# Linear attention with a routed feed-forward block on one core: two first loads exchanged between two DMA queues

## The chip, the cores and the metric

The kernel runs on one core of a Trainium2 chip. The core has a matrix engine (TensorE, PE in the profile), a vector engine (VectorE, DVE), a scalar engine (ScalarE, ACT), a general engine (GpSimd, POOL) and a synchronisation engine (SyncE, SP). The engines run their own instruction streams and wait for one another by semaphores. Transfers between the chip's memory and the core's SBUF are issued by an engine on its own DMA queue and carried by 16 DMA engines. The metric is the device time in microseconds; a version counts by the median of its runs.

## The reference

```python
x = A_x                                   # 1 x 2048 x 640, bf16
xn = _layernorm(x, axis=-1)
return x + _A_ref(xn, wqkv, wo) + _B_ref(xn, w_r, w_gate, w_up, w_down)

# _A_ref: linear attention, 32 heads of 20
q, k, v = split(xn @ wqkv)
phi = lambda t: where(t > 0, t + 1, exp(t)) + 1e-6
kv = einsum("bhsd,bhse->bhde", phi(k), v); z = phi(k).sum(s)
o = (phi(q) @ kv) / (phi(q) . z + 1e-6)
return o.reshape(B, S, D) @ wo

# _B_ref: the 8 rows with the largest xn @ w_r go through a gated feed-forward block
r = xn @ w_r;  idx = argsort(-r)[:8]
y = (silu(x_sel @ w_gate) * (x_sel @ w_up)) @ w_down * sigmoid(r_sel)
return xn + scatter_add(y at idx)
```

## The kernel before

The 2048 rows of x are 16 tiles of 128 rows. A tile of x is 128 x 640 in bf16, 160 KB. The kernel first runs through the tiles: normalise a tile (`ln_a`, `ln_b`: the two halves of the statistics on VectorE, lines 151 and 154; `ln_g`: their aggregate, line 157; `ln_r`: the inverse deviation by a logarithm and an exponential on ScalarE, lines 160 and 161; `ln_xn`: the normalised tile on VectorE, line 165), turn it, multiply it by the k columns of `wqkv` (`K`, line 208), apply phi (lines 224, 227, 243) and accumulate phi(k) times the normalised tile over all tiles (`G`, lines 248 and 253). Afterwards come q, the small matrices per head, the routed rows and the output.

Tiles 0 to 3 are turned on TensorE (`tr_mm`, line 174) and copied out of PSUM (`tr_cp`, line 181 on ScalarE, line 183 on VectorE). Later tiles are turned by a DMA (`tr_dma`). The order of the work on every engine is written out by hand: an engine does its instructions in the order in which the program names them.

The k columns come in two halves of 320, each 128 x 5 x 320 in SBUF and 400 KB: `wkh[0]` and `wkh[1]`. Each product of a tile with a half is five matmuls. Behind the columns of `wkh[1]` stands one column for the router weights `wr`: they are loaded as 5 rows of 128, transposed on TensorE (line 133) and copied by ScalarE (line 135), so that r comes out of the same products as k.

TensorE's first instructions, ahead of the first transposes of x, are filler products of a constant zero (`warm4`, line 121): one 512 wide, one 256 wide, then the transpose of `wr`, then another 512 wide. The filler of 32-bit numbers shows as two passes each.

What the change touches are the first loads, all issued through `ld` (line 103), so that the profile shows line 103 for every one. SyncE's queue holds x of tiles 0, 1, 2 and 3, then `wkh[1]`, then three loads of four tiles each. ScalarE's queue holds the table load of its functions (line 106), `wr` and `wkh[0]`. A transfer is not waited for by the engine that issues it; its users wait for its landing.

```python
ld(sp, XX[:, 0, 1, :], x_v[:, 0, :])
act.preload_act_table_set("natural_log_exp_and_others")
...
ld(act, wr[:], B_w_r.rearrange("(kc p) -> kc p", p=P))
ld(act, wkh[0], wqkv_v[:, :, D : D + HW])
ld(sp, XX[:, 1, 1, :], x_v[:, 1, :])
```

Of the kernel before, what the change touches and what calls it, by code (L numbers as in the profile page):

```python
# [9 lines left out]
D = 640  # L10
# [28 lines left out]
def kernel(  # L39
# [13 lines left out]
    pe, dve, act, pool, sp = nc.tensor, nc.vector, nc.scalar, nc.gpsimd, nc.sync  # L53

    x_v = A_x[0].rearrange("(t p) d -> p t d", p=P)
    out_v = out[0].rearrange("(t p) d -> p t d", p=P)
    wqkv_v = A_wqkv.rearrange("(kc p) n -> p kc n", p=P)
# [9 lines left out]
    def st(shape, dt, name, tag=None):  # L67
        return sb.tile(shape, dt, name=name, tag=tag or name)

    XX = st([P, T, 2, D], BF16, "XX")  # L70
# [27 lines left out]
    HW = 320  # L98
    wkh = [wk[:, :, 0:HW], wk[:, :, HW + 64 :]]


    def ld(eng, dst, src):
        eng.dma_start(dst, src)
# [3 lines left out]
    dve.memset(zero[:], 0.0)  # L107
    dve.memset(MVf[:], 0.0)
    wr = st([KC, P], BF16, "wr")
    ld(act, wr[:], B_w_r.rearrange("(kc p) -> kc p", p=P))  # L110
    ld(act, wkh[0], wqkv_v[:, :, D : D + HW])
    ld(sp, XX[:, 1, 1, :], x_v[:, 1, :])
    ld(sp, XX[:, 2, 1, :], x_v[:, 2, :])
    ld(sp, XX[:, 3, 1, :], x_v[:, 3, :])
    ld(sp, wkh[1][:, :, 0:HW], wqkv_v[:, :, D + HW : 2 * D])
# [824 lines left out]
```

## Time and profile before

| What | us |
|---|---|
| three runs: median, lowest, highest | 107.11, 106.8, 107.3 |
| the profiled execution | 106.82 |
| its span, first to last instruction | 105.1 |
| TensorE busy | 101.2 |
| VectorE busy | 82.3 |
| ScalarE busy | 69.3 |

The profile divides the span into instructions by engine. A row of the timeline gives the start, the time until the end of the last instruction that it merges, the engine, the line and the operation, the tiles written and read, the number of instructions, and in brackets the idle time before it with what ended that. PEld stands for the loads of a matrix into the array, which run beside products; SPq and ACTq are the issuing parts of SyncE and ScalarE. XX is the tile buffer of x, wk holds both halves of the k weights. In the tables of stages the columns are the stretch, its length, then busy time and number of instructions of PE, PEld, DVE, ACT and POOL, the granted clock of TensorE, the busy share of the DMA engines and GB/s. Queue q1 is SyncE's and q10 ScalarE's.

A busy TensorE row is no proof of full pace, since the ends of products are modelled; the starts are recorded.

### The profile page before, as it was taken

How to read it: one execution, taken by the hardware profiler on the slowest of the kernel's cores; microseconds unless marked ns; L12 is line 12 of the kernel's file. 1: busy time of each engine (PE TensorE's matmuls, PEld its weight loads, DVE VectorE, ACT ScalarE, POOL GpSimd, SP SyncE). 2: the span in 40 equal slices, each digit the busy share in tenths (PEclk: the TensorE clock that was granted, in tenths of full speed). 3: DMA queues.
4: the chain of work that ended last, by engine and by line, in shares of the span. 5: the costliest groups of instructions: out<-in, count | busy, mean ns of one | idle time of the engine just before them, and what ended most of it. 6: DMA issues, size and time to landing. Idle time of an engine off the chain costs nothing.

```text
span 105.1 us, 2557 instructions
## 1 busy us (share of the span) xinstructions
PE 101.2 (96%) x924; PEld 63.3 (60%) x924; DVE 82.3 (78%) x187; ACT 69.3 (66%) x171; POOL 17.3 (16%) x60
## 2 busy tenths in 40 slices
PE   6999999999999999999999999999999999999980
PEld 3346666666666666667556555655567767777760
DVE  1787999988888897873788985728988997888870
ACT  4289957666666666888596999969993997000000
POOL 7800000620000000000000683300002300000500
DMA  2899937334655765889998999921730125895343
GB/s 76 231 356 386 306 68 62 72 66 90 141 124 115 109 131 128 180 252 354 264 404 264 288 337 378 360 66 50 242 119 9 29 95 200 175 369 205 125 128 125
DMA packets 23024, 19.65 MB, mean 187 GB/s; under 512 B 10595, under 2 KB 21475, under 8 KB 23011
## 3 DMA queue, kind: packets, MB, share of 16 engines
q1 hardware_dynamic: 21880, 19.01, 62.6%
q10 hardware_dynamic: 842, 0.46, 1.8%
q8 instruction: 7, 0.11, 0.5%
q0 software_dynamic: 288, 0.01, 0.3%
q14 instruction: 7, 0.05, 0.2%
HBM read 13.80 MB, written 3.65 MB: 166 GB/s over the span
## 4 chain that ended last, share of the span: by engine, by line
PE 90%; DMA 5%; DVE 1%; issue 1%; ACT 1%; DVEq 0%
PE PS L208 21%; PE PS L474 21%; PE PS L739 20%; PE PS L248 16%; DMA wk<-in_A_wqkv_dram 5%; PE PS L253 3%; PE PS L695 2%; PE PS L655 1%; PE PS L538 1%; PE PS L717 1%; PE PS L267 1%; PE PS L174 1%; PE PS L666 1%; DVE o L752 1%; PE PS L618 1%
## 5 line engine op out<-in xcount | busy, mean ns | idle before, releaser
L208 PE MATMUL PS<-wk,xnT 128*128 128x320 bf16 (+1 forms) x160 | 25.3, 300 | 0.1
L248 PE MATMUL PS<-pk,XX 128*128 128x512 bf16 x80 | 23.5, 379 | 0.0
L474 PE MATMUL PS<-xnT,wq 128*128 128x512 bf16 x100 | 22.6, 380 | 0.0
L739 PE MATMUL PS<-Mb,pqT 128*128 128x320 bf16 (+4 forms) x165 | 22.1, 295 | 0.0
L224 ACT ACTIVATE ek<-PS 128x320 bf16<-128x320 f32 x32 | 14.1, 441 | 9.9 <-PE PS L208 9.9
L739 PEld LDWEIGHTS <-pqT 128*128 128x128 bf16 x165 | 15.9, 98 | 6.4 <-issue 0.3
L208 PEld LDWEIGHTS <-xnT 128*128 128x128 bf16 x160 | 15.3, 98 | 6.6 <-ACT xnT L181 0.2
L474 PEld LDWEIGHTS <-wq 128*128 128x128 bf16 x100 | 11.4, 118 | 9.1 <-issue 0.2
L243 DVE SCALAR_TENSOR_TENSOR pk<-ek,rk 128x640 bf16<-128x640 bf16 x16 | 13.1, 820 | 4.8 <-ACT rk L227 4.5
L529 DVE SCALAR_TENSOR_TENSOR pqT<-qe,qr 128x512 bf16<-128x512 bf16 x20 | 13.5, 683 | 2.1 <-ACT qr L481 2.0
L480 ACT ACTIVATE qe<-PS 128x512 bf16<-128x512 f32 x20 | 12.2, 609 | 3.3 <-PE PS L474 3.3
L253 PE MATMUL PS<-pk,XX 128*128 128x128 bf16 x64 | 14.0, 219 | 0.0
L227 ACT ACTIVATE rk<-PS 128x320 bf16<-128x320 f32 x32 | 14.0, 437 | 0.0
L248 PEld LDWEIGHTS <-XX 128*128 128x128 bf16 x80 | 7.8, 98 | 8.1
L481 ACT ACTIVATE qr<-PS 128x512 bf16<-128x512 f32 x20 | 12.2, 608 | 0.0
L748 DVE TENSOR_TENSOR o<-PS,XX 128x640 bf16<-128x640 f32 x11 | 9.0, 822 | 2.9 <-issue 1.3
L198 ACT ACTIVATE XX<-XX,MR,SR 128x640 bf16<-128x640 bf16 x11 | 9.4, 913 | 0.0
L151 DVE BATCH_NORM_STATS2 stats<-XX 128x6 f32<-128x320 bf16 x16 | 7.4, 461 | 2.2 <-DMA XX<-in_A_x_dram 2.2
L259 POOL MEMSET XX<- 128x1 bf16 x18 | 2.0, 117 | 35.4 <-DVE XX L165 15.2
L165 DVE TENSOR_SCALAR XX<-XX,MVf,SR 128x640 bf16<-128x640 bf16 (+2 forms) x17 | 7.2, 431 | 0.6 <-ACT SR L161 0.6
L154 DVE BATCH_NORM_STATS2 stats<-XX 128x6 f32<-128x320 bf16 x16 | 7.7, 480 | 0.0
L253 PEld LDWEIGHTS <-XX 128*128 128x128 bf16 x64 | 6.3, 98 | 0.8
(113 smaller groups left out, 95.3 us busy)
## 6 DMA issues: line engine op xcount, KB each, us to landing
out_dram<-o SPq DMA_DIRECT2D x15, 160.0 KB, 2.4
XX<-in_A_x_dram SPq DMA_DIRECT2D x3, 640.0 KB, 6.9
wg<-in_B_w_gate_dram SPq DMA_DIRECT2D x5, 384.0 KB, 9.0
wu<-in_B_w_up_dram SPq DMA_DIRECT2D x5, 384.0 KB, 6.2
wd<-in_B_w_down_dram SPq DMA_DIRECT2D x1, 1920.0 KB, 11.1
wv<-in_A_wqkv_dram SPq DMA_DIRECT2D x5, 160.0 KB, 3.0
wq<-in_A_wqkv_dram SPq DMA_DIRECT2D x1, 800.0 KB, 5.3
hi_d<-XX SPq DMA_DIRECT2D x1, 800.0 KB, 4.0
```

The source lines that it names most:

```text
L198: act.activation(XX[:, t, 1, :], XX[:, t, 1, :], AF.Identity, bias=MR[:, t : t + 1], scale=SR1[:, t : t + 1])
L208: pe.matmul(PS[:, b + h, off(t, h) : off(t, h) + w], lhsT=xnT[:, kc, t * P : (t + 1) * P], rhs=wkh[h][:, kc, 0:w], start=(kc == 0), stop=( ...
L224: act.activation(phis[t][0][:, h * HW : (h + 1) * HW], phi_src(t, h, b), AF.Exp)
L227: act.activation(phis[t][1][:, h * HW : (h + 1) * HW], phi_src(t, h, b), AF.Relu)
L243: dve.scalar_tensor_tensor(out=pk[:, t, :], in0=ek[:], scalar=1.0, in1=rk[:], op0=ALU.min, op1=ALU.add)
L248: pe.matmul(PS[:, a, :], lhsT=lhsT, rhs=pk[:, t, 0:512], start=(t == 0), stop=(t == T - 1),)
L253: pe.matmul(PS[:, 5, a * P : (a + 1) * P], lhsT=lhsT, rhs=pk[:, t, 512:D], start=(t == 0 and a == 0), stop=(t == T - 1), skip_group_check= ...
L474: pe.matmul(PS[:, bank, :], lhsT=by5(wq[:, kc, :])[:, m, :], rhs=xnT[:, kc, tb * TBLK : (tb + 1) * TBLK], start=(kc == 0), stop=(kc == KC ...
L480: act.activation(e, PS[:, bank, :], AF.Exp)
L481: act.activation(r, PS[:, bank, :], AF.Relu)
L529: dve.scalar_tensor_tensor(out=pqT[:, m, tb * TBLK : (tb + 1) * TBLK], in0=e, scalar=1.0, in1=r, op0=ALU.min, op1=ALU.add,)
L739: pe.matmul(PS[:, b, o : o + c1 - c0], lhsT=pqT[:, kc, t * P : (t + 1) * P], rhs=Mb[:, kc, c0:c1], start=(kc == 0), stop=(kc == KC - 1))
```

## The change

Three lines are written differently. x of tile 1 becomes the first transfer on ScalarE's queue, and `wr` the second. `wkh[0]` moves from ScalarE's queue to the second place on SyncE's, where x of tile 1 was. Nothing else differs, and the bytes are the same.

```diff
     wr = st([KC, P], BF16, "wr")
+    ld(act, XX[:, 1, 1, :], x_v[:, 1, :])
+    ld(sp, wkh[0], wqkv_v[:, :, D : D + HW])
     ld(act, wr[:], B_w_r.rearrange("(kc p) -> kc p", p=P))
-    ld(act, wkh[0], wqkv_v[:, :, D : D + HW])
-    ld(sp, XX[:, 1, 1, :], x_v[:, 1, :])
     ld(sp, XX[:, 2, 1, :], x_v[:, 2, :])
```

The head of ScalarE's stream, with what leaves it and what comes in (XX is x of tile 1, wk the first half of the k weights):

```order
 L935 UNCONDITIONAL_BRANCH
 L106 ACT_TABLE_LOAD
+L103 DMA XX<-in_A_x_dram 128x640
 L103 DMA wr<-in_B_w_r_dram 5x128
-L103 DMA wk<-in_A_wqkv_dram 128x5x320
 L135 COPY wk<-PS 128x5
```

The router weights are second now, and no weights of k are issued here.

The head of SyncE's stream; the four tiles that stood in one row are parted by the weights:

```order
 L935 UNCONDITIONAL_BRANCH
-L103 DMA XX<-in_A_x_dram 128x640 x4
+L103 DMA XX<-in_A_x_dram 128x640
+L103 DMA wk<-in_A_wqkv_dram 128x5x320
+L103 DMA XX<-in_A_x_dram 128x640 x2
 L103 DMA wk<-in_A_wqkv_dram 128x5x320
 L103 DMA XX<-in_A_x_dram 128x4x640 x3
```

The first half of the k weights stands behind tile 0 and ahead of tiles 2 and 3. The streams of TensorE, VectorE and GpSimd are the same in both kernels.

## The prediction

> **What bounds the kernel now.** I read the busy shares and the 40 slices first, then the chain of waits from the start, then the timeline of the first 10 us on each engine.
>
> ```profile
> PE 101.2 (96%) x924; PEld 63.3 (60%) x924; DVE 82.3 (78%) x187; ACT 69.3 (66%) x171; POOL 17.3 (16%) x60
> PE   6999999999999999999999999999999999999980
> 1.47 5.10 DMA wk<-in_A_wqkv_dram
> 6.57 0.04 issue
> 6.61 0.43 PE PS L208 x2
> 7.04 0.17 PE PS L174 x3
> 7.21 1.70 PE PS L208 x12
> ```
>
> TensorE is busy in every slice from the second on, and the chain from 6.61 us onward consists of TensorE pieces without a break. Before 6.61 it is the landing of the first half of the k weights, issued on ScalarE's queue at 1.47 and landed at 6.57. What the program can gain or lose by a new order of its first loads is therefore the moment at which TensorE's unbroken stretch begins, and whatever small holes follow until about 10 us. From there to 55 us nothing can absorb a shift:
>
> ```profile
> 6.60:10.00 3.40, 3.39 (x29) 2.15 (x28) 2.77 (x9) 3.05 (x12) 0.33 (x2) 1.00 1.06 377
> 10.00:55.00 45.00, 45.00 (x325) 28.45 (x325) 37.46 (x93) 33.16 (x100) 3.53 (x22) 1.00 0.70 170
> ```
>
> The second number of a row is its length, the third TensorE's busy time: 45.00 of 45.00. So I treat a shift at 10 us as a shift of the end, one for one.
>
> But the weights are not the only thing that stands just before 6.61. The chain names the last of several arrivals; the others are close behind:
>
> ```profile
> 3.17 0.49 DVE L151 BATCH_NORM_STATS2 stats<-XX 128x6 f32<-128x320 bf16 x1 [1.91 <-DMA XX<-in_A_x_dram]
> 3.97 0.48 DVE L151 BATCH_NORM_STATS2 stats<-XX 128x6 f32<-128x320 bf16 x1
> 5.16 1.05 DVE L165 TENSOR_SCALAR XX<-XX,MVf,SR 128x256 bf16<-128x256 bf16 x3
> 5.56 0.11 PEld L174 LDWEIGHTS <-XX 128*128 128x128 bf16 x2 [1.27 <-DVE XX L165]
> 5.89 1.10 ACT L181 COPY xnT<-PS 128x256 bf16<-128x256 bf16 x3 [0.16 <-PE PS L174]
> 6.33 0.10 PEld L208 LDWEIGHTS <-xnT 128*128 128x128 bf16 x1
> 6.54 0.49 DVE L151 BATCH_NORM_STATS2 stats<-XX 128x6 f32<-128x320 bf16 x1 [0.34 <-DMA XX<-in_A_x_dram]
> ```
>
> This is the chain of tile 0: x of tile 0 lands and VectorE starts its statistics at 3.17 after 1.91 us of waiting for it; the normalised tile comes at 5.16 and after; the first transpose follows at 5.56, its copy at 5.89, and the first k weight load into the array is done from 6.33. The product needs that load, 0.10 long, at least in part, so it could have started between 6.33 and 6.43; I take 6.39. The k weights therefore cost only 6.61 - 6.39 = 0.22 us (0.18 to 0.28). The second row matters as much: x of tile 1 shows no idle time before it, so nobody waited for that transfer. The last row shows x of tile 2, which did cost 0.34 us of VectorE.
>
> **The change, part by part.** The order of work on TensorE, VectorE and GpSimd is the same; only the first loads move. SyncE's transfers keep their places but for the second, where half of the k weights stands for x of tile 1. On ScalarE two transfers remain, x of tile 1 first. No step waits on more than before, and no issue becomes slower: the SyncE issues took about 0.43 us each for a tile and for half of the weights alike.
>
> ```profile
> 0.81 1.82 SPq L103 DMA_DIRECT2D XX<-in_A_x_dram  x4
> 0.84 0.59 ACTq L103 DMA_DIRECT2D wr<-in_B_w_r_dram  x1
> 1.27 0.42 SPq L103 DMA_DIRECT2D XX<-in_A_x_dram  x1
> 1.47 0.41 ACTq L103 DMA_DIRECT2D wk<-in_A_wqkv_dram  x1
> 2.67 0.43 SPq L103 DMA_DIRECT2D wk<-in_A_wqkv_dram  x1
> ```
>
> So x of tile 1 is issued at 0.84 instead of 1.27, the k weights at 1.27 instead of 1.47, the router weights at about 1.43 instead of 0.84. What the transfers then do to each other is read from this table of stages, whose last two columns are the busy share of the 16 DMA engines and GB/s:
>
> ```profile
> 1.70:2.60 0.90, 0.90 (x2) 0.34 (x1) 0.00 (x0) 0.39 (x1) 0.90 (x2) 1.00 0.73 209
> 2.60:3.10 0.50, 0.50 (x2) 0.34 (x1) 0.00 (x0) 0.00 (x0) 0.50 (x4) 1.00 1.01 271
> 3.10:3.60 0.50, 0.50 (x2) 0.00 (x0) 0.43 (x2) 0.00 (x0) 0.42 (x2) 1.00 0.47 90
> 3.60:4.60 1.00, 1.00 (x3) 0.60 (x3) 1.00 (x5) 0.18 (x2) 0.83 (x4) 1.00 0.90 215
> 4.60:6.60 2.00, 1.88 (x9) 0.46 (x8) 1.63 (x6) 1.71 (x6) 0.66 (x3) 1.00 1.09 347
> ```
>
> Added up, 0.188 MB have moved by 2.60, 0.324 by 3.10, 0.369 by 3.60, 0.584 by 4.60.
>
> *Tile 0 loses its head start: +0.40.* A tile of x is 0.164 MB. Before, it goes first and nearly alone, so it is through at about 1.70 + 0.164/0.209 = 2.49, and VectorE starts 0.68 later, at 3.17. Now tile 1 is issued 0.03 after it on the other queue. If the two alternate, both are through when 0.328 MB have moved, at about 3.14, and with the same 0.68 VectorE starts at 3.82: 0.65 later. If SyncE's packets all went first, it would be 0. Which of these is nearer is told by a stage in which both queues had work:
>
> ```profile
> q10 hardware_dynamic: 216, 0.14, 65.2%
> q1 hardware_dynamic: 63, 0.08, 24.8%
> ```
>
> These are packets, MB and share from 3.60 to 4.60 (q1 is SyncE's queue, q10 ScalarE's): neither is held back behind the other, so I go nearer to alternation than to no delay, but below its full price, since the pair need not both end at its last packet: 0.40, with 0 and 0.65 kept as ends. The Trainium skill, page "DMA: Bandwidth & Descriptors", section "Issuing engines are not separate DMA queues", says the same against this change: transfers started by different engines run on the same 16 DMA engines and interleave, and a second issuer saves only the time of issuing. By that rule the second queue brings tile 1 no bandwidth that tile 0 does not lose; the rows just shown agree.
>
> *The wait for the k weights goes: -0.22.* They are now behind 0.328 MB of x: 0.738 MB are through at 4.60 + (0.738 - 0.584)/0.347 = 5.04. Even with 1 us to land, that is ahead of the 6.79 (6.39 + 0.40) at which TensorE will ask for them. What hides this transfer is tile 0's own chain; without that cover the wait would return, since the landing now is 6.57.
>
> *x of tile 2: 0.* It has 0.902 MB up to its end, 5.52 by the same sum, 6.5 with the same 1 us. VectorE, which works through tiles 0 and 1 first (busy until 6.21 now, 6.61 then), will not wait for it. The 0.34 us that it waits now is where 0.34 of the 0.40 is taken up on VectorE; but TensorE and ScalarE, which start tile 0's products and copies later, are not helped by that.
>
> *Router weights: 0 to +0.5, taken as covered.* They move from the front of ScalarE's queue behind 0.164 MB. TensorE's queue holds their transpose ahead of a last filler product and of all transposes of x:
>
> ```profile
> 3.67 0.10 PEld L133 LDWEIGHTS <-wr 5*128 5x128 bf16 x1 [0.65 <-issue]
> 3.79 1.78 PE L121 MATMUL PS<-const-float32-0.0 128*128 128x512 f32 x2
> 4.80 0.77 PE L121 MATMUL PS<-const-float32-0.0 128*128 128x512 f32 x1
> 5.56 0.99 PE L174 MATMUL PS<-ident,XX 128*128 128x128 bf16 x7
> ```
>
> The transpose ran at 3.67 without a wait for data, and the filler behind it ends with the first transpose's start at 5.56: there is no slack in it. If the router weights land at 3.82, like the pair of tiles, the filler ends 0.15 later; at 4.3 (half a microsecond lost in the slow stage from 3.10 to 3.60), 0.6 later. Both run beside tile 0's delay, not behind it, so up to 0.40 is hidden.
>
> *After the start: 0.* VectorE's row at 9.49 waits 0.60 for ScalarE, whose work hangs on TensorE's products, so a later start is passed on through ScalarE; I let none be absorbed.
>
> ```profile
> 9.49 0.45 DVE L165 TENSOR_SCALAR XX<-XX,MVf,SR 128x640 bf16<-128x640 bf16 x1 [0.60 <-ACT SR L161]
> ```
>
> **Sum.** +0.40 - 0.22 + 0 + 0 + 0 = +0.18 us. The profiled execution took 106.82 (its span 105.1 and 1.7 around it), so it would be 107.00; the median of the three runs is 107.11, 0.29 above that, so I forecast a median of **107.3 us**. With the ends of the terms this case runs from 107.0 to 107.6. Half a per cent, 0.54 us, is about what a measurement of this kernel can tell from no change; this case stays within it.
>
> **Rivals.**
>
> *The start gets earlier.* If tile 0 keeps its place (delay 0 to 0.1), the 0.22 is gained, and the holes behind it may shrink as well, if tile 2 lands sooner: two weight loads of transposes wait for VectorE there.
>
> ```profile
> 8.82 0.11 PEld L174 LDWEIGHTS <-XX 128*128 128x128 bf16 x2 [0.25 <-DVE XX L165]
> 9.99 0.11 PEld L174 LDWEIGHTS <-XX 128*128 128x128 bf16 x2 [0.23 <-DVE XX L165]
> ```
>
> A product runs under most of each wait (a product's step is 0.14), so 0.1 of each, 0.2 in all, is an estimate of what can be won: 106.7 to 106.9, and with the luck of a sooner tile 0 at the very best 106.5. For it speaks that SyncE's issue comes 0.03 ahead; against it that the DMA engines are already 0.73 to 1.01 busy while tiles 0 and 1 move, so tile 1's packets must take time from tile 0's.
>
> *The weights' slow beginning meets tiles 0 and 1 (slower).* The rate falls to 90 GB/s from 3.10 to 3.60, just when the first packets of the k weights come. ScalarE's queue in the stages 1.70 to 2.60 and 2.60 to 3.60:
>
> ```profile
> q10 hardware_dynamic: 10, 0.00, 0.8%
> ```
>
> ```profile
> q10 hardware_dynamic: 58, 0.04, 26.0%
> ```
>
> These weights now stand directly behind tile 0 on SyncE's queue, issued 0.20 earlier, so the collapse may fall on the tails of tiles 0 and 1 and on the router weights. The loss is (271 - 90) x 0.5 = 0.09 MB, 0.33 us at 271 GB/s. Tile 0 then is 0.40 to 0.65 + 0.33 late, K's first product 0.5 to 0.76 later: 107.6 to 107.9. It decides from the point where tile 0 is ready for VectorE later than 3.9, or the router weights later than 4.4. Against it: the collapse may come from two queues that mix small and large rows, and then it moves or vanishes.
>
> *The array speeds up late (slower).* TensorE's filler is there ahead of the real work, and the array is slower at first:
>
> ```profile
> 1.83 0.34 PEld L121 LDWEIGHTS PS<-const-float32-0.0 128*128 128x128 f32 x1 [0.52 <-issue]
> 2.69 0.34 PEld L121 LDWEIGHTS PS<-const-float32-0.0 128*128 128x128 f32 x1 [0.52 <-issue]
> ```
>
> Between these two weight loads lies one pass of the 512-wide filler, 0.86; the last such pass began at 4.80 and was over by 5.56, 0.76 at most. If late router weights leave TensorE idle from 3.67 to 4.2, a speed-up that depends on unbroken work could come some 3 us later, and the products from 6 us on would start at half pace: of the 3.40 us of the stage 6.60 to 10.00 between 0 and 1.7 would be lost; I take 1.0, 108.3 us. Against it: the weight load at 3.67 has 0.65 without work before it already, and the granted-clock column reads 1.00 throughout. The Trainium skill, page "TensorE: Matmul & The Clock Gate", section "What's actually happening", has such a rule: half rate until one busy window of about 3.4 us has passed, the window running freely. By it an idle stretch inside the window could cost a whole further window; no row here shows where the window lies.
>
> *Nothing changes.* Tile 1 was not waited for, and the weights only for 0.22; with a delay of 0.2 to 0.25 the two cancel, 107.1. I count it with the forecast.
>
> **How the numbers follow.** Forecast with its neighbours 0.43; earlier start 0.15; the slow beginning of the weights 0.28; the late speed-up 0.14. Faster by over 0.5% is the better half of the second: 0.07. Slower by over 0.5% is the whole of the last, 0.24 of the 0.28, and 0.04 of the forecast's upper end: 0.42. The rest, 0.51, is within 0.5%. The range runs from 106.7 to 108.3: it leaves out the best of the second case and half of the last. The likeliest case alone has 107.0 to 107.6.
>
> **What would show it.** VectorE's first statistics (L151) at 3.4 to 3.8 instead of 3.17 show tile 0's delay; at 3.2 the first rival holds, at 3.9 or more the second. TensorE's first L208 product should follow its weight load without the wait, near 6.8, and the chain should begin with x of tile 0, not with the k weights. A wait before L133 that ends past 4.2 makes the router weights the cause. Steps of the first L208 products clearly above those of now (1.70 for 12, 0.14) show the late speed-up. I am wrong if the first product comes before 6.5 or after 7.1, or if the time moves while it stays put.

## The result and the profile after

The changed kernel takes 107.05 us (median of 20 runs, 106.76 to 108.47), the kernel before 106.62 in 20 runs of the same comparison (106.33 to 107.30). The ratio is 1.0037, with a 95% interval of 1.002 to 1.0054: 0.4% slower, 0.21 to 0.58 us. That lies inside the half per cent that the prediction allowed, and the whole interval lies above 1. Of the 20 runs of the changed kernel 16 lie from 106.76 to 107.20 and four from 107.97 to 108.47. Ratios here and below are of fast runs alone, those up to 1.5% above the fastest run of their kernel, so three of these four are left out. The profiled execution took 107.20, with a span of 105.5.

The head of the page of the changed kernel shows TensorE with the same work (the eight products fewer are records that the profile lacks) and a dent in the third of the 40 slices that was not there:

```profile
PE 100.5 (95%) x916; PEld 63.3 (60%) x924; DVE 82.3 (78%) x187; ACT 69.2 (66%) x171; POOL 17.5 (17%) x60
PE   6989999999999999999999999999999999999990
```

The chain of waits from the start (start, length, what) says what the dent is:

```profile
0.81 2.85 DMA XX<-in_A_x_dram
...
3.68 0.49 DVE stats L151
...
5.93 0.80 DVE XX L165 x2
...
6.77 0.28 PE PS L174 x2
7.06 0.27 PE PS L208 x2
...
7.50 1.70 PE PS L208 x12
...
11.96 0.22 PE PS L248
```

In the profile before, the landing of the k weights stood ahead of the first products. Now it is x of tile 0: its load, its statistics and its normalising, and no wait for weights at all. The timeline of the same execution shows both sides, VectorE's first statistics, then TensorE:

```profile
3.68 0.49 DVE L151 BATCH_NORM_STATS2 stats<-XX 128x6 f32<-128x320 bf16 x1 [2.42 <-DMA XX<-in_A_x_dram]
6.63 0.49 DVE L151 BATCH_NORM_STATS2 stats<-XX 128x6 f32<-128x320 bf16 x1
3.88 0.10 PEld L133 LDWEIGHTS <-wr 5*128 5x128 bf16 x1 [0.86 <-DMA wr<-in_B_w_r_dram]
4.00 1.66 PE L121 MATMUL PS<-const-float32-0.0 128*128 128x512 f32 x2
6.07 0.99 PE L174 MATMUL PS<-ident,XX 128*128 128x128 bf16 x7 [0.41 <-DVE XX L165]
6.89 0.43 PE L208 MATMUL PS<-wk,xnT 128*128 128x320 bf16 x2
11.79 0.38 PE L248 MATMUL PS<-pk,XX 128*128 128x512 bf16 x1
```

The statistics of tile 0 begin 0.51 later than before (3.68 against 3.17), the first product 0.28 later (6.89 against 6.61), the first product into phi(k) times x 0.15 later (11.79 against 11.64). Tile 2, which VectorE reaches at 6.63, is no longer waited for. The stages of the loads (stretch, length, busy times of five engines, granted clock, DMA share, GB/s):

```profile
1.70:2.60 0.90, 0.90 (x2) 0.34 (x1) 0.00 (x0) 0.38 (x1) 0.90 (x2) 1.00 0.72 137
...
3.10:3.60 0.50, 0.50 (x2) 0.00 (x0) 0.00 (x0) 0.00 (x0) 0.43 (x2) 1.00 1.02 322
```

The fall to 90 GB/s from 3.10 to 3.60 is gone (322), so more has been moved by 3.60; but from 1.70 to 2.60 it is 137 in place of 209. The other profiles of the two kernels agree: from 1.70 to 2.60 184 and 198 before, 175 and 112 after; from 3.10 to 3.60 200 and 233 before, 350 and 346 after. From 1.70 to 3.10 SyncE's queue moved 0.16 MB and ScalarE's 0.13 in the changed kernel, 0.32 and 0.01 in the kernel before. So the two tiles come in side by side, and at first at a lower rate together than tile 0 had with tile 1 behind it.

**Which execution stands for the kernel before?** The first pair of profiles alone would mislead, so both kernels were profiled twice more, in runs described below. The profiled executions of the kernel before took 106.82, 106.93 and 106.60; the third is the one at its median of 106.62. Its chain and its timeline begin so:

```profile
0.81 2.36 DMA XX<-in_A_x_dram
...
3.19 0.49 DVE stats L151
...
7.01 1.86 PE PS L208 x12
```

```profile
5.58 0.98 PE L174 MATMUL PS<-ident,XX 128*128 128x128 bf16 x7 [0.32 <-DVE XX L165]
6.41 0.43 PE L208 MATMUL PS<-wk,xnT 128*128 128x320 bf16 x2
11.44 0.38 PE L248 MATMUL PS<-pk,XX 128*128 128x512 bf16 x1
```

Here the first k weights land in time (at 5.88), the first product follows the chain of tile 0 at 6.41, and no wait for the first half of the weights is left that a new order could remove. Against this execution the changed kernel's first product at 6.89 (6.79 in its second profile) is 0.48 (0.38) late, and L248 at 11.79 (11.70) is 0.35 (0.26) late. The choice matters: the second profiles, 106.93 before and 106.98 after, are 0.25 apart at the first product (6.54 and 6.79) but only 0.05 at L248 (11.65 and 11.70), because that execution of the kernel before had a slow start of its own (e5) and lies 0.29 above the median of its runs.

**The rest of the difference** comes near the end. The whole spans of the first pair differ by 0.39 us (105.48 against 105.09), of which 0.15 is there at L248; from L248 to the first L474 both take 38.09. The other 0.24 arises in one place, the copies of the routed rows on GpSimd (L599) ahead of the feed-forward products (L695). Of the changed kernel, GpSimd and then TensorE:

```profile
65.28 0.40 POOL L599 COPY xsT<-xnT 128x5 bf16 x1 [0.47 <-issue]
66.30 0.35 POOL L599 COPY xsT<-xnT 128x5 bf16 x1 [0.63 <-issue]
67.95 1.00 PE L695 MATMUL PS<-wg,xsT 128*32 128x384 bf16 x20 [0.15 <-POOL xsT L599]
```

The same rows of the kernel before:

```profile
65.16 0.37 POOL L599 COPY xsT<-xnT 128x5 bf16 x1 [0.49 <-issue]
65.91 0.91 POOL L599 COPY xsT<-xnT 128x5 bf16 x2 [0.38 <-issue]
67.56 1.00 PE L695 MATMUL PS<-wg,xsT 128*32 128x384 bf16 x20
```

From one copy to the next it is 1.02 us in the first and 0.75 in the second, and TensorE waits for the last copy in the first alone. Between the two copies GpSimd fetches the number of the next row (L598). GpSimd's idle time ahead of the second copy, in brackets, is 0.63 here and 0.38 before; over all fourteen profiles it is 0.29 to 0.63, and 0.49 and 0.47 in the second profiles of the two kernels. Long and short ones come with other orders of the loads too, so I count it as chance; three profiles of each kernel do not show that the two are equal on average.

That nothing else differs can be added up. In the eleven profiles whose granted clock stays at 1.00 (all but e7 to e9), take from the time of the execution the start of the first L248 product and the stretch from the first L474 to the first L695 product, which holds the fetches (17.80 to 18.07). What is left is 77.33 to 77.39 in all eleven. So executions of these kernels differ before L248 and in the fetches, and nowhere else by more than 0.06.

### The profile page after: what moved, and what is told of

Read it like the earlier page. It is cut to its first block, busy times and chain, and to the rows that moved or that the text cites. A ratio compares the mean times of both kernels' runs of the same rounds, so it can differ in the third digit from the quotient of the medians.

```text
span 105.5 us, 2548 instructions
## 1 busy us (share of the span) xinstructions
PE 100.5 (95%) x916; PEld 63.3 (60%) x924; DVE 82.3 (78%) x187; ACT 69.2 (66%) x171; POOL 17.5 (17%) x60
## 4 chain that ended last, share of the span: by engine, by line
PE 80%; issue 5%; DVE 3%; POOLq 3%; DMA 3%; ACT 3%; POOL 1%; DVEq 0%
PE PS L208 21%; PE PS L739 19%; PE PS L248 15%; PE PS L474 12%; PE PS L253 4%; DMA XX<-in_A_x_dram 3%; POOLq L598 3%; ACT qr L481 2%; PE PS L695 2%; PE PS L174 1%; PE PS L717 1%; PE PS L267 1%; DVE stats L151 1%; DVE XX L165 1%; PE PS L666 1%
## 5 line engine op out<-in xcount | busy, mean ns | idle before, releaser
L248 PE MATMUL PS<-pk,XX 128*128 128x512 bf16 x75 | 22.7, 379 | 0.0
L474 PE MATMUL PS<-xnT,wq 128*128 128x512 bf16 x97 | 22.4, 380 | 0.2
L474 PEld LDWEIGHTS <-wq 128*128 128x128 bf16 x100 | 11.4, 118 | 9.1 <-issue 0.2
L248 PEld LDWEIGHTS <-XX 128*128 128x128 bf16 x80 | 7.8, 98 | 8.1
L165 DVE TENSOR_SCALAR XX<-XX,MVf,SR 128x640 bf16<-128x640 bf16 (+2 forms) x17 | 7.2, 432 | 0.6 <-ACT SR L161 0.6
```

The costliest lines, as they stand in the source:

```text
L248: pe.matmul(PS[:, a, :], lhsT=lhsT, rhs=pk[:, t, 0:512], start=(t == 0), stop=(t == T - 1),)
L474: pe.matmul(PS[:, bank, :], lhsT=by5(wq[:, kc, :])[:, m, :], rhs=xnT[:, kc, tb * TBLK : (tb + 1) * TBLK], start=(kc == 0), stop=(kc == KC ...
```

## The experiments

All edits are to the first loads (e8 and e12 also move instructions of the engines), against the changed kernel unless said. Times are medians with their range; ratios are to the kernel before, run beside them (its medians were 106.6 to 106.7).

**e1: router weights ahead of tile 1.** Is it the tile beside tile 0 that delays tile 0, or the k weights behind it?

```diff
-    ld(act, XX[:, 1, 1, :], x_v[:, 1, :])
-    ld(sp, wkh[0], wqkv_v[:, :, D : D + HW])
     ld(act, wr[:], B_w_r.rearrange("(kc p) -> kc p", p=P))
+    ld(act, XX[:, 1, 1, :], x_v[:, 1, :])
+    ld(sp, wkh[0], wqkv_v[:, :, D : D + HW])
```

> The change with the two transfers of ScalarE's queue in the other order: router weights first, x of tile 1 second. Tile-0 theory (the loss is x of tile 1 sharing the DMA engines with x of tile 0): tile 1 is issued about 0.43 us later, as before the change, so VectorE's first statistics return to 3.2 to 3.3 (3.68 with the change, 3.17 before), the first L208 product comes at 6.4 to 6.5 (6.89 and 6.61), and the time is 0.2 to 0.5 us under the change's, at or a little under before. Router theory (the loss is the late router weights): the transpose L133 starts at 3.67 again, the time returns to before's or a little under as well, but VectorE's first statistics stay near 3.6. Rest theory (the loss is GpSimd's fetching of rows at 61 to 67 us and has nothing to do with the loads): no change against the change, ratio about 1.004.

Measured: 108.60 (107.70 to 110.55), ratio 1.0159 (1.0127 to 1.0191). VectorE:

```profile
3.29 0.49 DVE L151 BATCH_NORM_STATS2 stats<-XX 128x6 f32<-128x320 bf16 x1 [2.04 <-DMA XX<-in_A_x_dram]
5.59 0.49 DVE L151 BATCH_NORM_STATS2 stats<-XX 128x6 f32<-128x320 bf16 x1 [1.41 <-DMA XX<-in_A_x_dram]
```

With tile 1 issued 0.6 us later, and the k weights where the change has them, tile 0 has most of its head start back (3.29): the tile issued together with it was the cause, not the weights behind it. The time expected from that, at or under the kernel before, did not come: the loss is elsewhere, and larger. Tile 1, issued at 1.46 behind the k weights of 1.26 on the other queue, lands 4.11 us after its issue. From 2.60 to 3.60 SyncE's queue moved 0.12 MB and ScalarE's 0.02, both together 123 and then 165 GB/s. VectorE's order has the first statistics of tile 1 ahead of the aggregate and the normalising of tile 0, so tile 0 waits 1.41 for tile 1, and the first product comes at 8.02.

**e2: router weights on GpSimd's queue.** How much does the landing of the router weights matter, if nothing else is moved?

```diff
+    ld(pool, wr[:], B_w_r.rearrange("(kc p) -> kc p", p=P))
     ld(act, XX[:, 1, 1, :], x_v[:, 1, :])
     ld(sp, wkh[0], wqkv_v[:, :, D : D + HW])
-    ld(act, wr[:], B_w_r.rearrange("(kc p) -> kc p", p=P))
```

> The change, but with the router weights issued by GpSimd on its own queue at the start, so that they no longer stand behind x of tile 1; tile 1 stays first on ScalarE's. Tile-0 theory: L133 starts at 3.67 but nothing else moves; VectorE's first statistics near 3.6 to 3.7, first L208 product near 6.85 to 6.9, ratio to before 1.003 to 1.005, as with the change. Router theory: L133 at 3.67 and the time back at before's or under it, ratio 1.000 or less. Rest theory: ratio 1.004.

Measured: 108.66 (107.52 to 109.10), ratio 1.0208 (1.0187 to 1.0228). The router weights did not come sooner, as expected, but later: the 1.2 KB issued by GpSimd at 1.37 landed at 5.14, 3.77 us after. TensorE in this profile, the shortest of its runs (107.52):

```profile
5.18 0.17 PE L133 MATMUL PS<-ident,wr 5*128 5x5 bf16 x1 [1.44 <-DMA wr<-in_B_w_r_dram]
5.29 1.13 PE L121 MATMUL PS<-const-float32-0.0 128*128 128x512 f32 x2
7.19 0.43 PE L208 MATMUL PS<-wk,xnT 128*128 128x320 bf16 x2
```

VectorE had tile 0 at 3.74, as in the changed kernel (3.58 to 3.71). Here the start is set by the router weights and the filler behind them: the transposes follow the filler at 6.42 and wait for nothing else. That is 0.9 us over the kernel before; the other four runs, 108.48 to 109.10, were not profiled, so the rest of their loss stays open. TensorE had stood idle for 1.44 ahead of the transpose, and the filler behind it ran at its quickest all the same.

**e3: everything in one queue.** Router weights alone on ScalarE's queue; tile 0, tile 1 and the k weights in SyncE's.

```diff
-    ld(act, XX[:, 1, 1, :], x_v[:, 1, :])
-    ld(sp, wkh[0], wqkv_v[:, :, D : D + HW])
     ld(act, wr[:], B_w_r.rearrange("(kc p) -> kc p", p=P))
+    ld(sp, XX[:, 1, 1, :], x_v[:, 1, :])
+    ld(sp, wkh[0], wqkv_v[:, :, D : D + HW])
```

> Router weights alone on ScalarE's queue, and x of tile 0, x of tile 1, the first half of the k weights, x of tile 2 one behind the other on SyncE's. Tile-0 theory: x of tile 0 goes alone, VectorE's first statistics at 3.1 to 3.2, the k weights are through by about 5.2, the first L208 product at 6.35 to 6.45, 0.2 us ahead of before; tile 2 is in by 6.2, so the holes behind shrink: ratio to before 0.996 to 0.999. Router theory: the same L133 as before, and nothing else to gain but the wait for the k weights, 0.998. Rest theory: ratio 1.004 unless GpSimd's chain happens to be quick.

Measured: 107.40 (107.20 to 107.88), ratio 1.0076 (1.0057 to 1.0095). VectorE's first row, then TensorE:

```profile
3.08 0.49 DVE L151 BATCH_NORM_STATS2 stats<-XX 128x6 f32<-128x320 bf16 x1 [1.82 <-DMA XX<-in_A_x_dram]
3.79 1.22 PE L121 MATMUL PS<-const-float32-0.0 128*128 128x512 f32 x2
6.30 0.43 PE L208 MATMUL PS<-wk,xnT 128*128 128x320 bf16 x2
8.94 0.71 PE L208 MATMUL PS<-wk,xnT 128*128 128x321 bf16 x4 [0.89 <-DMA wk<-in_A_wqkv_dram]
```

With tile 1 behind it, tile 0 keeps its place (first statistics at 3.08), the k weights are in time (6.03), and the first product at 6.30 is the earliest of all profiles. The kernel is slower all the same, against what was expected: one queue brings the second half of the k weights only at 8.90, and TensorE stops 0.89 us for it. This bound stands close behind the first in the kernel before too: there the second half lands at 8.12 in the third profile, and its 12 products take 1.86 in place of 1.70.

**e4: router weights behind the k weights.**

```diff
     ld(sp, wkh[0], wqkv_v[:, :, D : D + HW])
-    ld(act, wr[:], B_w_r.rearrange("(kc p) -> kc p", p=P))
+    ld(sp, wr[:], B_w_r.rearrange("(kc p) -> kc p", p=P))
```

> The change with the router weights later still: third on SyncE's queue, behind x of tile 0 and the first half of the k weights. They should land at about 5.0 to 5.3 (3.84 with the change). Tile-0 theory: in the change the filler behind L133 ends about 0.3 us before tile 0 is ready, so the first 0.3 us of lateness are free and the rest is paid: L133 at 5.1 to 5.3, filler over at 6.9 to 7.1, first L208 product at 7.7 to 7.9, 0.8 to 1.0 us behind the change's; the time 0.6 to 1.0 above the change's. Router theory: every 0.1 of lateness is paid, 1.2 to 1.4 above the change. If unbroken work is what speeds the array up, the idle stretch of 1.4 us also costs half pace for up to 3 us: another 1 us and steps of 0.27 in the first L208 products.

Measured: 108.79 (107.02 to 109.40), ratio 1.0125 (1.0077 to 1.0173). The profile is of the longest run:

```profile
5.40 0.18 PE L133 MATMUL PS<-ident,wr 5*128 5x5 bf16 x1 [1.66 <-DMA wr<-in_B_w_r_dram]
5.51 2.08 PE L121 MATMUL PS<-const-float32-0.0 128*128 128x512 f32 x2
8.27 0.72 PE L208 MATMUL PS<-wk,xnT 128*128 128x320 bf16 x2
```

Two losses stand on top of each other. The filler behind late router weights holds up the transposes, and the products themselves run slowly: a row of two takes 0.72 in place of 0.43. By their starts, the steps become normal only at about 10.4.

**e5, e6: both kernels again.** No edit: e5 is the kernel before, e6 the changed one.

> The kernel before once more, for a second profile of it. Start theory (all of the lost time is lost in the first loads): the first L248 product at 11.5 to 11.8 and the last L474 product about 65.5 us behind it, as in the first profile, ratio 1.000. Fetch theory (part of it is the length of one row fetch on GpSimd at about 65 us, which differs from run to run whatever the kernel): the hole ahead of the L695 products, 0.07 in the first profile of before, is anywhere from 0.04 to 0.3 here.

> The changed kernel once more, for a second profile and its spread on another chip. Start theory: first L208 product 0.2 to 0.5 later than before's on the same chip, and the first L248 product later by all of the difference in time, ratio 1.003 to 1.006. Fetch theory: the first L248 product 0.1 to 0.2 later than before's, and the rest of the difference lies at the L695 products and is not steady.

Measured: e5 106.64 (12 runs, 106.53 to 107.35), ratio 1.0001 (0.998 to 1.0021); e6 107.08 (7 runs, 106.96 to 107.18), ratio 1.0038 (1.0025 to 1.0052). The difference of 0.4 us repeats. A row of the chain of e5, the kernel before:

```profile
3.86 2.00 PE PS L121 x2
```

Its chain starts with neither the weights nor tile 0, but with the filler; the pair of passes behind the router weights takes 2.00 us here and holds up the first transpose to 5.66. In six profiles with the transpose of the router weights at the same 3.68, the timeline gives this pair 1.22 (e3), 1.48 (third profile of before), 1.65 (e9), 1.78 (the first of before, up to the next start) and 2.08 (here and e1). Three of them are of the kernel before, so when the array speeds up differs from one execution to the next, with nothing in the program to account for it.

**e7, e8: tiles 0 and 1 by halves.** If tile 0 loses its head start because it shares the DMA engines with tile 1, half of it could go on each queue, with the halves of tile 1 behind. e8 also puts the transpose of the router weights behind all of the filler.

```diff
-    ld(sp, XX[:, 0, 1, :], x_v[:, 0, :])
+    ld(sp, XX[0:64, 0, 1, :], x_v[0:64, 0, :])
...
-    ld(act, XX[:, 1, 1, :], x_v[:, 1, :])
+    ld(act, XX[64:P, 0, 1, :], x_v[64:P, 0, :])
+    ld(sp, XX[0:64, 1, 1, :], x_v[0:64, 1, :])
+    ld(act, XX[64:P, 1, 1, :], x_v[64:P, 1, :])
```

```diff
     warm4(256)
-    pe.transpose(PS[:, 3, :].bitcast(BF16)[:, 0:KC], wr[:], ident[0:KC, 0:KC])
     warm4(512)
-    act.copy(wkh[1][:, :, HW], PS[:, 3, :].bitcast(BF16)[:, 0:KC])
+    pe.transpose(PS[:, 3, :].bitcast(BF16)[:, 0:KC], wr[:], ident[0:KC, 0:KC])
...
     tr_cp(0, 0, 0, act)
+    act.copy(wkh[1][:, :, HW], PS[:, 3, :].bitcast(BF16)[:, 0:KC])
```

> The change, but x of tiles 0 and 1 in halves of 64 rows, one half of each on either queue: both queues carry tile 0 first, then tile 1; the k weights stand behind that on SyncE's queue, the router weights on ScalarE's. The bytes ahead of each other are as in the change, only tile 1 no longer takes a share while tile 0 is moving. Tile-0 theory: VectorE's first statistics at 3.1 to 3.3 in place of 3.68; the router weights land near 3.8 as in the change, so L133 comes at 3.8 to 3.9 and the filler ends at 5.7 to 5.8; the first L208 product at 6.5 to 6.65, as before or 0.1 sooner, ratio to before 0.998 to 1.001. Rival (what delays tile 0 is not tile 1 but the slow beginning of the k weights, issued sooner): VectorE's first statistics stay at 3.6 or later, ratio 1.004.

> The same split, and the transpose of the router weights moved behind the filler on TensorE, with its copy behind the first copy of tile 0 on ScalarE, so that a late landing of the router weights no longer holds the filler up. Tile-0 theory: VectorE's first statistics at 3.1 to 3.3, filler over before 5.5, first L208 product at 6.3 to 6.45, 0.2 sooner than before; the second half of the k weights, landing at 8.0, then is the next wait (0.05 to 0.1): ratio to before 0.996 to 0.999. If the array's pace depends on unbroken filler, no run is among the ones that take 1.3 us longer. Router theory: the same ratio, but reached only here and not in the split alone.

Measured: e7 109.66 (108.40 to 110.03), ratio 1.0226 (1.0186 to 1.0265); e8 108.42 (107.67 to 109.47), ratio 1.0138 (1.0106 to 1.0169). Splitting fails at its own aim, and neither expectation for it came true. A stage of e7's loads:

```profile
1.70:2.60 0.90, 0.90 (x2) 0.34 (x1) 0.00 (x0) 0.39 (x1) 0.90 (x2) 1.00 0.35 78
```

The issue of half a tile took 0.57 to 0.86 us, that of a whole one in the first place 0.40; 78 GB/s move where the six profiles of the two kernels have 112 to 209, and the first statistics begin at 3.56, hardly earlier than in the changed kernel. Its second half of tile 1 lands at 5.52 and the router weights at 5.73. In e8 the filler is over by 4.7 and an idle stretch follows; the stages behind it:

```profile
6.60:8.60 2.00, 1.93 (x14) 1.25 (x15) 1.97 (x6) 1.64 (x6) 0.20 (x2) 0.65 1.05 320
8.60:10.60 2.00, 2.00 (x9) 1.16 (x8) 1.07 (x4) 1.43 (x6) 0.00 (x0) 0.50 1.04 378
```

Here the granted clock falls to 0.50, with a TensorE that is busy all the time and gets through 9 instructions in place of 14. This is not the whole loss: only two of e8's six runs have a mean granted clock under 0.99 (109.18 and 109.47), and the others took 107.67 to 108.72 at 1.00. In the profile the second half of the k weights also lands late, at 9.37. e8 changes too much at once to say which of these costs what, so it does not tell whether the router weights alone are worth moving.

**e9: the second half of the k weights on ScalarE's queue.** e3 had the best start and a late second half. Against the kernel before, with SyncE's queue in e3's order; the second half is issued by ScalarE once it has copied the router weights.

```diff
-    ld(act, wkh[0], wqkv_v[:, :, D : D + HW])
     ld(sp, XX[:, 1, 1, :], x_v[:, 1, :])
+    ld(sp, wkh[0], wqkv_v[:, :, D : D + HW])
...
-    ld(sp, wkh[1][:, :, 0:HW], wqkv_v[:, :, D + HW : 2 * D])
...
     act.copy(wkh[1][:, :, HW], PS[:, 3, :].bitcast(BF16)[:, 0:KC])
+    ld(act, wkh[1][:, :, 0:HW], wqkv_v[:, :, D + HW : 2 * D])
```

> The single-queue order (router weights alone on ScalarE's queue; x of tiles 0 and 1, the first half of the k weights, x of tile 2 and on, on SyncE's), but the second half of the k weights taken out of SyncE's queue and issued by ScalarE after its copy of the router column, at about 4.1. In the single-queue run TensorE began at 6.30 and then stood still for about 1 us until that half landed at 8.9. If that late half alone made it slower: it lands before 8.0 here, the first L208 product stays at 6.3 to 6.4, the stop of 1 us is gone and the ratio to before is 0.996 to 0.999, ahead of both kernels. If a single queue simply carries less in the first 6 us: the half lands after 8.2, the stop is shorter but still there, ratio 1.000 to 1.005.

Measured: 113.70 (112.59 to 115.16), ratio 1.0607 (1.0561 to 1.0653). A row of its chain, and TensorE:

```profile
3.90 9.21 DMA wk<-in_A_wqkv_dram
```

```profile
13.16 1.23 PE L208 MATMUL PS<-wk,xnT 128*128 128x321 bf16 x4 [4.89 <-DMA wk<-in_A_wqkv_dram]
```

Issued at 3.90 on a queue with nothing else left in it, this transfer landed 9.21 us later, and neither expectation had a stop of 4.89. In SyncE's queue it stood ahead of the three loads of four tiles. Here two of these were issued before it on the other queue, at 3.24 and 3.72, and landed before it, at 9.26 and 11.82. From 4.60 to 8.00 ScalarE's queue moved 5 packets of 1082. So it came behind them, although they were in another queue.

**e10, e11: both kernels a third time, e12: aggregate first.** e10 is the kernel before, e11 the changed one, one run each. e12 takes from VectorE the other thing that holds tile 0 up, the statistics of tile 1 in the middle of its own.

```diff
     ln_b(0)
-    ln_a(1)
     ln_g(0)
+    ln_a(1)
     ln_b(1)
```

> The kernel before, a third profile. The two so far (106.82 and about 106.9) lie above its median of 106.6. If the wait for the first half of the k weights (0.22 in the first profile) is not there in usual runs: here the first L208 product comes under 6.5 and the first L248 product at 11.35 to 11.55. If the usual runs only have shorter row fetches on GpSimd: L248 at 11.65 again and the stretch from the first L474 product to the first L695 product at 17.80 to 17.85.

> The changed kernel, a third profile. If tile 0's delay is steady: VectorE's first statistics at 3.5 to 3.8, the first L208 product at 6.75 to 6.95, the first L248 product at 11.65 to 11.85, as in the two so far.

> The change with one instruction of VectorE moved: the aggregate of tile 0 ahead of the first statistics of tile 1. Tile-0 theory (VectorE's chain from x of tile 0 to its normalised tile is what the start now hangs on): the aggregate comes 0.3 to 0.4 sooner, the normalised tile and the first L208 product 0.2 to 0.3 sooner (6.55 to 6.7 against 6.8 to 6.9), the time 0.1 to 0.25 under the change's, ratio to before 1.001 to 1.003. Rival (the router weights and the filler behind them set the start): the first transpose comes no sooner than 1.9 after the router weights' landing, the first L208 product moves by less than 0.1, ratio 1.004.

Measured: e10 106.60, shown above, with L248 at 11.44, the sign of its first reading, and 17.80 from the first L474 to the first L695 product, the short fetches of its second: both play a part. e11 107.92, close to the four longer runs; tile 0 is ready as expected, at 3.71, and everything behind it later. TensorE of e11:

```profile
4.24 2.07 PE L121 MATMUL PS<-const-float32-0.0 128*128 128x512 f32 x2
...
6.99 0.73 PE L208 MATMUL PS<-wk,xnT 128*128 128x320 bf16 x2
...
12.72 0.38 PE L248 MATMUL PS<-pk,XX 128*128 128x512 bf16 x1
```

The first product comes at 6.99, only 0.10 later than in the first profile after, but L248 0.93 later: the products ran slowly until about 8.9. Its chain from the start runs through the filler and not through tile 0. The router weights had landed at 4.08, the latest of the changed kernel's three profiles (3.74 and 3.84 in the others).

e12: 107.10 (12 runs, 106.97 to 108.53), ratio 1.005 (1.0023 to 1.0076), no gain over the changed kernel. Its profile is of one of its two longest runs, 108.42:

```profile
4.16 2.08 PE L121 MATMUL PS<-const-float32-0.0 128*128 128x512 f32 x2
6.17 1.23 PE L174 MATMUL PS<-ident,XX 128*128 128x128 bf16 x7
```

There VectorE has tile 0's first normalised piece (L165 begins at 5.82) before TensorE is through with its filler, and the first transpose waits for nothing on VectorE: the filler behind the router weights has become the last arrival. Whether that is so in its ordinary runs of 107.1 as well was not profiled, so this experiment does not settle what is next after tile 0 there.

## Why the prediction came out as it did

The forecast of 107.3 and its side were right: the measured 107.05 lies in the range of the likeliest case (107.0 to 107.6), and the rise, 0.43 us, within half a per cent. The place was right too: the first product at 6.89 in the stretch named for it, and the chain led by x of tile 0. In the pair of executions that it was worked out on, L248 came 0.15 later, against +0.18. But sizes of single terms were not right, and that they partly cancelled is luck.

- **Tile 0 loses its head start, +0.40: the cause right, the size 0.1 low.** First statistics at 3.17, 3.14 and 3.19 before, at 3.68, 3.58 and 3.71 after: +0.49 between the means. It is tile 1 that takes it: in six profiles with tile 1 issued beside tile 0, it is 3.58 to 3.80; in e1, e3 and e9, with tile 1 later or behind, 3.08 to 3.29. Up to 3.10 the two queues had moved 0.16 and 0.13 MB, so they share nearly evenly. The section of the Trainium skill cited in the prediction, that queues of different engines interleave on the same 16 DMA engines, agrees with these numbers for two tiles issued together. Sharing is not all of it: the prediction kept the 209 GB/s of the first stage for both tiles, and it was 112 to 175.
- **The wait for the k weights goes, -0.22: true of one execution of three.** This is the term that was mis-sized. The wait was read correctly in the profile at hand (the weights landed at 6.57), and it went, as predicted; but in the two other profiles of the kernel before they landed at 5.91 and 5.88 and nobody waited for them. So the term is 0 in two of three executions, among them the one at the median. The slow stage from 3.10 to 3.60, 90 GB/s in that profile, was 200 and 233 in the others.
- **x of tile 2: 0, right for its landing** (VectorE no longer waits for it; in the two other profiles of before it did not either). But the term *after the start: 0* was wrong by 0.13, the part of the delay that is absorbed between the first product and L248: 5.03 us there before, 4.90 after. The first of the two weight loads that waited for VectorE, 0.25 at 8.82 before, has no wait now; the second still has 0.18. In the third profile of before the holes are elsewhere (12 products in 1.86 for 1.70), and as large. The prediction had these holes in view, but gave them only to the rival of the earlier start.
- **Router weights, taken as covered: right for the ordinary run.** They landed at 3.74 to 4.08, the bounds having been 3.82 and 4.3; the filler behind them ends by 5.66 and the first transpose waits 0.41 for VectorE. The reading that the filler before had no slack holds for e5, but in the third profile the first transpose waits 0.32 for VectorE. In the profiles of e2 and e4, where the router weights land at 5.14 and 5.36, the cover is used up and the transposes follow the filler.
- **Base.** The median of three runs before, 107.11, stood 0.49 above that of 20 runs, these three among them, 106.62. The prediction added 0.29 for it. So 107.3 was near the result with a rise that was 0.25 too small on a base that was 0.49 too high.

With the terms as measured, on the third profile of before: 0.49 (3.68 - 3.19) at VectorE, 0.48 at the first product, 0.35 at L248; with the second profile of the changed kernel 0.39, 0.38 and 0.26. That is 0.26 to 0.35 of the 0.43 measured, and in its interval; the remainder is of the size by which the fetches on GpSimd differ.

**The rivals.** *The start gets earlier* did not occur: tile 0 did not keep its place; only its small term, the holes, was real. *The slow beginning of the weights meets tiles 0 and 1* did not occur: 322 GB/s from 3.10 to 3.60, tile 0 ready at 3.68 and not at 3.9. The slow stage goes with the order of the loads: in the six profiles with tile 1 issued beside tile 0 it is 322 to 357 GB/s there, in the three of before and in e1, e3 and e9 90 to 233. Two queues with rows of two sizes, the reason that the prediction offered, are not needed for it: e3 has both in one queue and shows 133. *The array speeds up late* did not decide the median, but it exists: e11 is such an execution of the changed kernel, 0.93 later at L248 than the first one, where 1.0 had been taken. The array's speed-up comes at another time in each execution: the filler pair behind the router weights took 1.13 to 2.08 us. The Trainium skill, page "TensorE: Matmul & The Clock Gate", section "What's actually happening", says that one kernel shows different numbers of slow products from run to run, because the window runs freely; the trace agrees with the first and cannot show the second. The granted clock reads 1.00 in all these starts and shows none of it; only in e7 to e9, after a later idle stretch, does it read 0.50 to 0.75.

**What stays open.** Whether the later router weights make the late speed-up more frequent. The times speak for it: no run of the kernel before, in any comparison, was above 107.46, against 4 in 20, 0 in 7 and e11 of the changed kernel, 2 in 12 of e12, and five of e4's six were above 108.3. But e5, an execution with early router weights, was slow until about 6.9 too, e2's profile shows a quick array behind an idle stretch of 1.44, and no run varied the idle stretch alone with the rest kept. Nor was it found out why two tiles issued together move more slowly at first, and why the k weights start slowly in the other orders. e1, e3 and e9 give tile 0 its place back, but each with a new wait elsewhere, so no run shows the 0.43 us going away with tile 0's delay alone. No version tried beats the kernel before.

## What to carry to other kernels

A load issued on a second queue at the same moment as the first one was paid for by the first here: before moving it forward, ask what the transfer beside it feeds, and here that was the head of the longest chain, while the load moved forward was waited for by nobody. A wait of 0.2 us in one profile is not yet a term of the sum: look at a second execution before counting on its removal. And behind a first bound look for the next arrivals on every engine; here five (tile 0, two halves of the k weights, router weights with filler, the array's own speed-up) stood close behind one another, and no move of one of them won anything.

## What was not expected of the hardware

- A second queue did not carry a transfer past what had been issued earlier on the first. The second half of the k weights, issued at 3.90 beside loads of four tiles issued before it, landed after 9.21 us (e9), where it took 5.4 in SyncE's own order; a tile issued 0.20 behind the k weights landed after 4.11 us (e1). In both the rows differ in size as well (1280 bytes for a tile, 640 for the weights), so the order of issue is an explanation that fits and not one that was tested.
- 1.2 KB issued by GpSimd took 3.77 us to land (e2). Issued by ScalarE at 0.84 as its first transfer, the same bytes were in by 2.49 (kernel before).
- A transfer of 64 rows took longer to issue than one of 128 (0.57 to 0.86 us in e7, against 0.40 for the first tile of the changed kernel).
- The wait for one row number on GpSimd, between the same two copies, is 0.29 to 0.63 us from one execution to another; with it the stretch from the first L474 to the first L695 product is 17.80 to 18.07.
